# A decode attention block with a gated MLP: weight loads in fewer, longer pieces

## The chip, the cores and the metric

The kernel runs on one core of a Trainium2 chip. The core has five instruction queues: TensorE (PE, with its weight loads as PEld), VectorE (DVE), ScalarE (ACT), GpSimd (POOL) and SyncE (SP). Sixteen DMA engines move data between the chip's memory (HBM) and the on-chip memory (SBUF, 128 partitions). Transfers are put into DMA queues by SP, ACT and POOL. The metric is the device time of one launch in microseconds (us); smaller is better.

## The reference, cut to what matters

One token passes through two branches that a scalar gate mixes. Branch A is attention over a cache of 4096 keys and values for 32 heads of 128 numbers, with a projection before (wq) and after (wo). Branch B is an MLP with a squared ReLU. All inputs are bf16.

```python
g = sigmoid((x * gate_w).sum(-1))                     # x: 1 x 512
q = (x @ wq).reshape(32, 128)                         # wq: 512 x 4096
p = softmax(einsum("hd,hkd->hk", q, k_cache) * 128 ** -0.5)
o = einsum("hk,hkd->hd", p, v_cache)                  # caches: 32 x 4096 x 128
a = o.reshape(4096) @ wo                              # wo: 4096 x 512
h = relu(x @ w1 + b1) ** 2                            # w1: 512 x 1376
b = h @ w2 + b2                                       # w2: 1376 x 512
out = g * a + (1 - g) * b
```

The caches are 64 MB of the roughly 79 MB that must be read; wq and wo are 4 MB each, w1 and w2 1.4 MB each.

## The kernel before, in words

The kernel is written engine by engine with semaphores; no scheduler reorders it.

**The stream.** SP issues nearly all loads, in this order: wq in four transfers (L249, L257), keys of seven heads, and then in a loop over heads the values of head h and the keys of head h+7 (L268, L263). Each of those is 1 MB, 128 partitions of 8 KB. Eight buffers hold keys (Kt), eight hold values (Vt); from the ninth head on, SP waits until a buffer is free (L261, L262, L267) before it issues. After the values of head 8 it issues w1 in four transfers of 2752 bytes per partition (L286). Behind the last values come a part of wo (wob, wox) and w2 (w2a, w2b), L289 to L293.

**The work on a head.** DVE multiplies half of the keys with the query and sums (L631, sixteen instructions a head). PE transposes the other half (L428), ACT moves it out of PSUM (L362) and PE takes the scores (L439). A softmax over groups of four heads follows, and PE multiplies with the values (L464).

**The buffer W.** wq fills W, 128 partitions of 32 KB. Its product with x is made in eight steps spread over the first 22 heads (L406, semaphore s_qps). When the eighth is done, W is free, and 92 of its partitions are filled with 92 rows of wo of 32 KB each, enough for 23 heads. These loads are the strips. `place` turns a strip into a first partition, a step and a count of partitions.

- POOL issues the fourteen strips in `RUNS` (L319) after it has waited for s_qps: two of 24 rows, one of 3, one of 7 and ten of 2, 78 rows in all.
- SP issues the five strips in `FIRST` (L280) between the values of heads 20 to 24: four of 3 rows and one of 2, 14 rows.

The strips carry `max_dma_last_dim=8192`, which cuts a row of 32 KB into pieces of 8 KB. In the built program a strip of 24 rows then is a pattern of 24 x 4 x 4096 elements: two counting dimensions, rows and pieces, over a contiguous run.

**The turn.** The code keeps account of which DMA engine a strip's rows go to. `RUNS` names for each strip a first engine e and a number of engines k (4 and 12 for the 24-row strips, two rows each; 4 and 3; 7 and 2; 9 and 7, and so on). `turns` follows a cursor modulo 16: after a strip it stands at e + k. Where the next strip is to start elsewhere, a filler transfer of d tiny rows (L316, a pattern of d x 2 x 8 elements, 32 bytes a row) moves it on by d, or it is reset to zero (L313) and moved from there. `place` puts the rows of engine e into partitions 32+4e to 35+4e, or from 4e (engines 0 to 7) or 64+4e (engines 8 to 15), four each. So engine e always fills the same eight partitions.

**The end.** PE multiplies the strips with the attention result (L508), DVE takes nine of the 32 column blocks (L681), PE adds wob, wox, w2a and w2b to the sum `acc` (L526, L532, L547), and DVE, PE and SP finish and store the output.

## Time and profile before

| | before |
|---|---|
| time of three runs, us | 196.81, 196.83, 196.99 (median 196.83) |
| profiled execution, us | span 195.4; the page gives it no other time |
| DVE busy | 139.5 us, 71% |
| PE busy | 132.8 us, 68% |
| bytes read from HBM | 78.32 MB |
| mean rate of the DMA engines | 403 GB/s |
| last input lands (w2a) | 191.87 us after the span's start |

The span runs from the first to the last instruction; the median lies 1.4 us above it, which is what stands around the program on the chip. "Busy tenths" are the busy share in 40 equal slices of the span, 9 meaning 90% or more. A DMA line such as `x32, 1024.0 KB, 27.1` tells the number of transfers, the size of each, and the median us from issue to landing. The trace also holds a record of each packet on the DMA engines: queue, start, duration and size, but not which of the 16 engines it was.

### The profile page before, as it was taken

The numbers are of one execution on the slowest core, as the hardware profiler recorded it, in microseconds if no ns is written. First come the engines' busy times: TensorE is split into PE (matmuls) and PEld (weight loads), VectorE is DVE, ScalarE is ACT, GpSimd is POOL, SyncE is SP. The second block draws the span as 40 slices with busy tenths as digits, with TensorE's granted clock in tenths as the row PEclk, the third lists the DMA queues.
The fourth block names the chain that finished last, engine by engine and source line by source line (L and its number), as shares of the span: only waits on it lengthen the run. The fifth ranks groups of instructions, "written<-read, shape, count | busy, mean of one in ns | idle before, by whom it ended". The sixth has DMA issues, their size and how long they took to land.

```text
span 195.4 us, 6571 instructions
## 1 busy us (share of the span) xinstructions
PE 132.8 (68%) x2409; PEld 117.3 (60%) x2409; DVE 139.5 (71%) x1151; ACT 79.4 (41%) x148; POOL 29.9 (15%) x53
## 2 busy tenths in 40 slices
PE   0128657597986857906797771568998677787774
PEld 0106527476686647606667761568997667776664
DVE  0307999999998687707877773577769999958510
ACT  2105838456563536403347330633068333612000
POOL 2000000000000000000009950000089760000000
PEclk9999966667555665555555555555555555555555
DMA  6999999999999999999999999999999999999991
GB/s 227 420 426 424 424 418 424 411 421 426 416 411 423 418 421 407 420 421 421 418 421 419 411 416 416 406 409 413 408 419 421 426 409 421 419 423 414 416 382 57
DMA packets 12717, 78.76 MB, mean 403 GB/s; under 512 B 2489, under 2 KB 2715, under 8 KB 3356
## 3 DMA queue, kind: packets, MB, share of 16 engines
q1 hardware_dynamic: 11134, 75.77, 94.0%
q0 software_dynamic: 1536, 2.56, 3.5%
q8 instruction: 19, 0.31, 0.7%
q14 instruction: 14, 0.11, 0.2%
q10 hardware_dynamic: 14, 0.01, 0.0%
HBM read 78.32 MB, written 0.00 MB: 401 GB/s over the span
## 4 chain that ended last, share of the span: by engine, by line
DMA 59%; DVE 22%; PE 9%; SPq 6%; issue 3%; ACT 0%
DMA Kt<-in_A_k_cache_dram 42%; DVE Kt L631 19%; DMA w2a<-in_B_w_dram 12%; DMA W<-in_A_wq_dram 6%; SPq L268 4%; PE KP L428 3%; PE pX L482 2%; DVE S L631 1%; SPq L263 1%; PE pQ L406 1%; PE pX L478 1%; PE pX L547 1%; PE pS L439 1%; DVE dg L646 1%; DVE S L637 0%
## 5 line engine op out<-in xcount | busy, mean ns | idle before, releaser
L631 DVE CUSTOM_DVE_ANT_0 Kt<-Kt,qb 128x128 bf16<-128x128 bf16 x512 | 113.3, 290 | 23.4 <-DMA Kt<-in_A_k_cache_dram 23.4
L362 ACT ACTIVATE kT<-KP 128x1024 bf16<-128x1024 bf16 x64 | 61.8, 1021 | 68.4 <-PE KP L428 68.4
L428 PE MATMUL KP<-ident,Kt 128*128 128x128 bf16 x512 | 55.2, 294 | 32.0 <-DMA Kt<-in_A_k_cache_dram 32.0
L428 PEld LDWEIGHTS KP<-ident,Kt 128*128 128x128 bf16 x512 | 47.9, 137 | 34.4 <-DMA Kt<-in_A_k_cache_dram 33.6
L631 DVE DVE_READ_ACCUMULATOR2_ANT S<- 128x1 f32 x512 | 41.4, 81 | 0.0
L439 PE MATMUL pS<-qcol,kT 128*128 128x1 bf16 x512 | 19.0, 167 | 11.1 <-DVE S L637 11.1
L439 PEld LDWEIGHTS pS<-qcol,kT 128*128 128x128 bf16 x512 | 18.4, 106 | 13.2 <-DVE S L637 13.2
L316 POOL DMA_DIRECT2D xb<-in_B_w_dram x9 | 5.3, 592 | 100.3 <-PE pQ L406 100.3
L406 PE MATMUL pQ<-W,xb 128*128 128x512 bf16 x32 | 14.5, 609 | 6.4 <-DMA W<-in_A_wq_dram 6.4
L464 PEld LDWEIGHTS pO<-E,Vt 128*128 128x128 bf16 x512 | 15.4, 104 | 1.1 <-issue 0.8
L464 PE MATMUL pO<-E,Vt 128*128 128x1 bf16 x512 | 16.0, 165 | 0.0
L334 POOL TENSOR_SCALAR_AFFINE_SELECT w_sb<-w_sb 24x36 bf16<-24x36 bf16 (+5 forms) x19 | 11.0, 577 | 2.7
L354 ACT ACTIVATE qb<-pQ 128x512 bf16<-128x512 f32 x8 | 4.7, 591 | 14.8 <-PE pQ L406 14.8
L406 PEld LDWEIGHTS pQ<-W,xb 128*128 128x128 bf16 x32 | 3.6, 130 | 10.9 <-issue 10.9
L373 ACT ACTIVATE E<-S,nM 128x32 bf16<-128x32 f32 x32 | 9.9, 309 | 0.3
L464 PE MATMUL pQ<-E,Vt 128*128 128x1 bf16 x256 | 8.1, 165 | 2.3 <-DMA Vt<-in_A_v_cache_dram 2.0
L464 PEld LDWEIGHTS pQ<-E,Vt 128*128 128x128 bf16 x256 | 7.7, 104 | 2.6 <-issue 2.5
L464 PEld LDWEIGHTS pX<-E,Vt 128*128 128x128 bf16 x256 | 7.9, 105 | 0.7 <-issue 0.6
L464 PE MATMUL pX<-E,Vt 128*128 128x1 bf16 x256 | 8.1, 166 | 0.0
L319 POOL DMA_DIRECT2D W<-in_A_wo_dram x14 | 7.8, 563 | 0.0
L617 DVE CAST qcol<-pQ 128x4 bf16<-128x4 f32 x8 | 1.2, 152 | 8.5 <-PE pQ L414 8.5
L637 DVE COPY S<-pS 128x16 f32<-128x16 f32 x32 | 5.4, 169 | 2.2 <-PE pS L439 2.2
(85 smaller groups left out, 93.5 us busy)
## 6 DMA issues: line engine op xcount, KB each, us to landing
Kt<-in_A_k_cache_dram SPq DMA_DIRECT2D x32, 1024.0 KB, 27.1
Vt<-in_A_v_cache_dram SPq DMA_DIRECT2D x32, 1024.0 KB, 27.2
W<-in_A_wq_dram SPq DMA_DIRECT2D x4, 1024.0 KB, 7.8
W<-in_A_wo_dram POOLq DMA_DIRECT2D x2, 768.0 KB, 13.0
w_sb<-in_B_w_dram SPq DMA_DIRECT2D x4, 344.0 KB, 22.9
Kt<-in_A_wo_dram SPq DMA_DIRECT2D x1, 1024.0 KB, 21.5
w2a<-in_B_w_dram SPq DMA_DIRECT2D x1, 1024.0 KB, 23.4
W<-in_A_wo_dram POOLq DMA_DIRECT2D x10, 64.0 KB, 23.4
```

The costliest lines, as they stand in the source:

```text
L268: eng.dma_start(Vt[:, h % NV, :], v_h[h, :, :]).then_inc(s_v[h % NV], 16)
L316: eng.dma_start(dm[0:d, sent, :, 0:8], src[:, :, 0:8]).then_inc(s_dm[sent], 16)
L319: eng.dma_start(W[p:p + st * (k - 1) + 1:st, :], woa_v[q:q + k, :], max_dma_last_dim=8192).then_inc(s_wp[n], 16)
L334: eng.affine_select(out=part, in_=part, compare_op=ALU.not_equal, fill=1.0, base=-st * q, pattern=[[st, 4], [-1, st * (k - 1) + 1]], chann ...
L362: eng.activation(kT[:, h % 2, j * HB * 128:(j + 1) * HB * 128], KP[n % 3][:, :], ACT.Copy).then_inc(s_ev, 1)
L373: eng.activation(E[:, h % NE, :], S[:, h % NS, :], ACT.Exp, bias=nM[:, h:h + 1], scale=SCALE, accum_out=RS[:, h:h + 1]).then_inc(s_e, 1)
L406: mm = eng.matmul(pQ[:, :], xb[:, t, :], wq_sb[:, t, c * 512:(c + 1) * 512], start=(t == 0), stop=(t == 3))
L428: mm = eng.transpose(KP[n % 3][:, y * 128:(y + 1) * 128], Kt[:, h % NK, b * 128:(b + 1) * 128], ident[:, :])
L439: mm = eng.matmul(S2[:, y:y + 1], kT[:, h % 2, y * 128:(y + 1) * 128], qcol[:, h:h + 1], start=True, stop=True)
L464: mm = eng.matmul(O(h, h + 1), Vt[:, h % NV, b * 128:(b + 1) * 128], E[:, h % NE, b:b + 1], start=(b == 0), stop=(b == NB - 1))
L631: ins = eng.tensor_tensor_reduce(kb, kb, qb[:, h * 128:(h + 1) * 128], 1.0, 0.0, ALU.mult, ALU.add, S[:, h % NS, b:b + 1])
L637: eng.tensor_copy(S[:, h % NS, XB:NB], S2).then_inc(s_cp, 1)
```

## The change: what it does

Three groups of loads are issued with longer contiguous pieces. The bytes, their places in SBUF and the order of the transfers stay.

- wq: two transfers of 16 KB per partition in place of four of 8 KB; PE waits for two semaphores in place of four.
- w1: one transfer of 11,008 bytes per partition in place of four of 2752.
- the strips of wo, on POOL and on SP: no cap, so that each row is one piece of 32 KB. In the built program a strip of 24 rows is now 24 x 16384 elements: one counting dimension over a contiguous run. `RUNS`, `turns` and the fillers stay as they were.

```diff
-        nc.sync.dma_start(wq_sb[:, 0, :], wq_v[:, 0, :]).then_inc(s_wq[0], 16)
+        nc.sync.dma_start(wq_sb[:, 0:2, :], wq_v[:, 0:2, :]).then_inc(s_wq[0], 16)
...
-            for t in range(1, 4):
-                eng.dma_start(wq_sb[:, t, :], wq_v[:, t, :]).then_inc(s_wq[t], 16)
+            eng.dma_start(wq_sb[:, 2:4, :], wq_v[:, 2:4, :]).then_inc(s_wq[1], 16)
...
-                    eng.dma_start(W[p:p + st * (k - 1) + 1:st, :], woa_v[q:q + k, :],
-                                  max_dma_last_dim=8192).then_inc(s_wr, 16)
+                    eng.dma_start(W[p:p + st * (k - 1) + 1:st, :], woa_v[q:q + k, :]).then_inc(s_wr, 16)
...
-                    for t in range(4):
-                        eng.dma_start(w1_sb[:, t, :], w1_v[:, t, :]).then_inc(s_w1, 16)
+                    eng.dma_start(w1_sb[:, :, :], w1_v[:, :, :]).then_inc(s_w1, 16)
...
-                eng.dma_start(W[p:p + st * (k - 1) + 1:st, :], woa_v[q:q + k, :],
-                              max_dma_last_dim=8192).then_inc(s_wp[n], 16)
+                eng.dma_start(W[p:p + st * (k - 1) + 1:st, :], woa_v[q:q + k, :]).then_inc(s_wp[n], 16)
...
-                eng.wait_ge(s_w1, 64)
+                eng.wait_ge(s_w1, 16)
```

More of the change, by code (lines that the diff above doesn't have):

```diff
@@ L195, in bass_gated_mix__gqa_block_cached__dense_activation_squared_relu__decode_kernel @@
         s_b = sem("s_b")
-        s_wq = [sem(f"s_wq{t}") for t in range(4)]
+        s_wq = [sem(f"s_wq{t}") for t in range(2)]
         s_w1 = sem("s_w1")
@@ L396, in _ @@
             eng.matmul(Z, onesf[0:1, :], zp[:, :], start=True, stop=True).then_inc(s_z, 1)
-            for t in range(4):
+            for t in range(2):
                 eng.wait_ge(s_wq[t], 16)
```

## The prediction

> **What bounds the kernel now.** I read the page's rows for DMA by slices and queues first, then a table of five stretches, then the end of the chain, then DMA issues and the waits.

> ```profile
> span 195.4 us, 6571 instructions
> ...
> DMA  6999999999999999999999999999999999999991
> ...
> DMA packets 12717, 78.76 MB, mean 403 GB/s; under 512 B 2489, under 2 KB 2715, under 8 KB 3356
> ...
> q1 hardware_dynamic: 11134, 75.77, 94.0%
> q0 software_dynamic: 1536, 2.56, 3.5%
> q8 instruction: 19, 0.31, 0.7%
> q14 instruction: 14, 0.11, 0.2%
> ```

> All sixteen DMA engines work through 38 of 40 slices. Queue 1 is what SP issues, queue 0 what POOL issues (2.56 MB: its 78 rows of wo). Queues 8 and 14 fetch instructions: 19 packets of 16 KB and, mostly, packets of 8 KB.

> ```profile
> core 0: us, PE busy (x) PEld busy (x) DVE busy (x) ACT busy (x) POOL busy (x), PEclk, DMA share, GB/s
> 0.00:13.00 13.00, 0.84 (x6) 0.70 (x6) 1.93 (x10) 1.83 (x4) 1.25 (x9) 1.00 0.87 350
> 13.00:102.00 89.00, 64.06 (x1018) 52.41 (x1019) 72.98 (x662) 44.73 (x72) 0.00 (x0) 0.63 1.01 419
> 102.00:146.00 44.00, 31.70 (x565) 30.72 (x566) 29.28 (x248) 17.59 (x34) 16.60 (x25) 0.50 1.02 413
> 146.00:189.50 43.50, 33.30 (x744) 31.06 (x741) 34.74 (x229) 15.27 (x39) 12.09 (x20) 0.50 1.01 417
> 189.50:195.40 5.90, 2.86 (x82) 2.46 (x81) 0.54 (x3) 0.00 (x0) 0.00 (x0) 0.50 0.31 100
> ```

> DMA share is 1.01 or 1.02 in each stretch from 13 to 189.5 us, at 413 to 419 GB/s, while DVE and PE leave a fifth to a third free. The limit is the service time of the DMA engines.

> ```profile
> 168.51 23.36 DMA w2a<-in_B_w_dram
> 191.87 0.14 issue
> 192.01 0.99 PE pX L547 x32
> ```

> The chain ends with an input that was issued 23.4 us before it landed, so it stood in a queue; 3.5 us of work follow. The packet records show how the engines finish: about 16 packets are in flight until 189.7 us, about 9 at 191.0, four at 192.0, and the last data packet ends at 192.56. Some four engines set the end, 2.8 us behind the first to finish. So the question is what the change does to the busiest engine.

> ```profile
> Kt<-in_A_k_cache_dram SPq DMA_DIRECT2D x32, 1024.0 KB, 27.1
> Vt<-in_A_v_cache_dram SPq DMA_DIRECT2D x32, 1024.0 KB, 27.2
> W<-in_A_wq_dram SPq DMA_DIRECT2D x4, 1024.0 KB, 7.8
> ```

> Keys and values wait in the queue for most of 27 us: no issue instruction is on the path.

> **Part 1, wq and w1.** The packet records give the price of a piece: median 46 ns for 1 KB, 109 for 2752 bytes, 312 for 8 KB. That is a line of 37 ns per KB and about 7 ns per piece. Each engine serves 8 of the 128 partitions, so wq falls from 32 pieces to 16 on an engine and w1 from 32 to 8: 40 pieces x 7 ns = 0.28 us less. Five transfers fewer, each with a closing record of 9 ns on every engine, give 0.05. SP issues two wq transfers fewer, some 0.4 us each in its timeline, and three w1 transfers fewer of 0.4 to 2.1 us; that is worth nothing, since the keys behind wq queue up anyway (SP's first value transfer already takes 2.07 us to issue) and 23 to 27 us of backlog cover w1. If the cover were gone it would be a gain of under 1 us at the start. PE needed all four parts of wq before its first product, so two semaphores cost nothing; the same holds for w1.

> Pieces of data over 8 KB are not in the trace. The nearest rows are the instruction queues: 0.7% x 16 x 195.4 us / 19 = 1.15 us per packet of 16 KB, 0.2% x 16 x 195.4 / 14 = 0.45 us per packet of 8 KB. So the two ends are 0.62 us for 16 KB (the line) and about 1.1 us (that row). By the second, wq costs 16 x (1.09 - 0.62) = +7.4 us on each engine. I take the line: three sizes of data lie on it, and instruction packets come singly and go to another place.

> **Part 2, the strips: the price of a piece.** A row now is one piece, not four: 3 x 7 ns less per row. POOL's 312 packets of 8 KB took 97.9 us together, 0.314 each, so a row is 1.256 us of one engine's time.

> **Part 3, the strips: which engine.** This decides. By the kernel's own account (first engine e, number of engines, two rows each in the 24-row strips) engine 0 now carries 3 POOL rows and 5 SP rows, engine 1 two and five, engines 7, 8 and 15 eight rows each and the others one to six. Eight rows, 10.0 us, is the most, on four engines, and four engines end last. The trace agrees with the account where it can: in the first 0.35 us of strip data twelve 8 KB packets of queue 0 start, the 12 engines of the first strip.

> That account was kept for strips with two counting dimensions, rows and pieces. The fillers have two as well, 2 x 8 out of rows of 16, which cannot fold into one although 32 bytes would need no second. After the change the strips have one. No POOL transfer with one is in this trace, so I bound it. At one end it is dealt as before: with eight rows on the busiest engine the whole change is -(40 + 24) x 7 ns - 0.05 = -0.5 us. At the other end the cursor plays no part and every POOL strip starts at engine 0. Engines 0 and 1 then get 2 + 2 rows of the 24-row strips, 1 of the 3-row, 1 of the 7-row and 10 of the 2-row strips: 16, plus their 5 from SP: 21. The excess over eight is 13 x 1.256 = 16.3 us, less (40 + 63) x 7 ns and 0.05 for the shorter lists, 0.8: +15.5 us. I take the second end: the fillers' odd shape makes sense only if the dealing depends on the second dimension.

> [...]

> **Part 4, the strips: whose partitions.** Engine 1's sixteen POOL rows then all go to partitions that the code gives to other engines (4 to those of engine 5, and so on), and those engines write keys and values there at the same time. The trace has one load that does not keep to the map: w2b, 96 partitions, six to an engine in order. While it lands, at 190.0 to 190.3 us, packets of 1 KB take up to 91 ns, not 46 (1.98 times), and packets of 2 KB 129 on average, not 84 (1.53 times). So a row out of place costs between nothing more and 0.98 x 1.256 us more. Engine 1 had seven rows, so its 14 more give the same 16.3 over the old end. Sixteen rows at 1.53: + 16 x 0.53 x 1.256 = 10.6 us; at 1.98: +19.7. I take 1.53, a mean over that stretch.

> Sum: 16.3 + 10.6 - 0.8 = +26.1 us. The tail of 3.5 us and the 1.4 us between span and median stay. On the profiled 195.4 that is 221.5; on the median of 196.83 it is 222.9, say 223. Can it hide? Other engines would wait, not help: a key transfer counts as landed when its last engine is done. DVE and PE stall there and, with 20 to 35% free, keep up again afterwards; engine 1 always has the backlog. The strips are first read at 175.6 us, long after they land.

> **Rivals.** (a) The dealing stays, and only piece prices change: 196.83 - 0.5 = 196.3, faster. For it: same bytes, same order, the whole 0.5 us on the busiest engine. Against: the shape of the fillers. It decides if the engine with most rows keeps eight. Its gain is near what measurement tells, 0.2% or 0.4 us, so a third of this case falls within that. [...]

> (b) The strips pile up, but rows out of place cost nothing extra: 196.83 + 15.5 = 212.3. For it: the slow packets at 190 us could be due to the mix of small packets. It is the low part of my case.

> (c) The dealing stays, but long pieces run like the 16 KB instruction packets, 0.068 us per KB: wq +7.4, eight rows 8 x (2.17 - 1.25) = +7.4, w1 8 x (0.73 - 0.44) = +2.3; together 214. Against: the line through three sizes.

> **How the numbers follow.** Piled up, with any price for rows out of place: 0.84, from 212 to 232 by part 4, with a us or three beyond each end for the count of rows that the busiest engine had before; that is its own range, 209 to 236. Rival (b) is 0.2 of that. Rival (c): 0.03. Rival (a): 0.13, of which 0.09 is faster by over 0.2% and 0.04 within 0.2%. Slower: 0.84 + 0.03 = 0.87. The range 209 to 236 leaves out (a) and some 0.07 for long pieces on top of the pile or a higher price.

> **What would show it.** DMA packets fall by some 1000 (256 of wq, 384 of w1, 276 of strips and closing records). The DMA share falls clearly below 1 in the part after 107 us, because fourteen engines wait for two; the mean rate falls from 403 to about 350 GB/s. The waits of DVE L631 and PE L428 for keys (23.4 and 32.0 us) each grow by about the whole loss, behind 107 us and not before. Queue 0 shows packets far above 1.25 us per 32 KB if rows out of place cost. The first product starts at 13.2 us as before; if it starts near 20, long pieces are slow in themselves. Wrong would be: a DMA share that stays at 1 to the end with a time near 196.

## The result and the profile after

The changed kernel takes 230.43 us (median of four runs, 230.35 to 230.88), the kernel before 196.91 us beside it. The ratio is 1.1705, with a 95% interval of 1.1688 to 1.1721: 33.5 us slower. The forecast was 223 us, from 209 to 236.

The page of the changed kernel, its rows for DMA:

```profile
span 228.9 us, 6565 instructions
...
DMA  6999999999999999999999999989999999696100
GB/s 238 447 408 422 421 420 420 420 418 422 412 420 421 421 415 424 420 420 368 274 259 222 256 372 322 372 302 367 358 384 378 361 399 358 256 412 244 56 40 16
DMA packets 11187, 78.76 MB, mean 344 GB/s; under 512 B 1875, under 2 KB 2101, under 8 KB 2230
...
q1 hardware_dynamic: 10372, 75.77, 85.6%
q0 software_dynamic: 768, 2.56, 4.6%
```

The bytes are the same. The rate is that of before, around 420 GB/s, for 18 slices, and then falls, to 222 GB/s in slice 22. The engines nevertheless look busy there: until slice 35 most digits are 9. Queue 0, POOL's, moves the same 2.56 MB, but its packets occupy 4.6% of 16 x 228.9 us, 168 us, where before 3.5% of 16 x 195.4 us made 109 us. So between 105 and 155 us the engines are busy at work that got slower, and at the end most of them have nothing to do. A table by stretches shows the two:

```profile
core 0: us, PE busy (x) PEld busy (x) DVE busy (x) ACT busy (x) POOL busy (x), PEclk, DMA share, GB/s
107.00:157.00 50.00, 13.93 (x265) 13.50 (x265) 16.54 (x149) 9.15 (x17) 8.18 (x15) 0.50 0.98 293
157.00:207.00 50.00, 34.20 (x625) 32.59 (x625) 36.22 (x287) 18.29 (x34) 15.65 (x21) 0.50 0.95 368
207.00:226.20 19.20, 14.03 (x381) 13.32 (x382) 7.76 (x16) 1.50 (x9) 0.00 (x0) 0.50 0.22 82
```

The first stretch is POOL's strips: a DMA share of 0.98, but 293 GB/s. In the last 19 us the share is 0.22. The packet records have two to three packets in flight on average from 210 to 219 us and about one at 222; the last data packet ends at 226.0 us. From 221 us on it is one engine: followed back packet by packet, it works without a gap to 226.0 us, mostly at 309 ns a piece of 8 KB.

SP's own strips tell which engines are late. By the code's account their 14 rows go to engines 0 and 1 (five each) and 2 (four). The 14 packets of 32 KB form three series: one of four that starts at 158.5 us, and two of five that start at 171.0 and 175.7. In the kernel with a cap of 16 KB on POOL's strips (below) the three series start within 1.6 us, at 140.0 to 141.5. So engines 0 and 1 stand 12.5 and 17 us behind engine 2, in one order or the other.

The chain ends as before, with w2a:

```profile
199.51 25.71 DMA w2a<-in_B_w_dram
225.22 0.14 issue
225.35 0.99 PE pX L543 x32
```

The waits for keys take up the whole loss; DVE waits 32.6 us more than before and PE 35.5. Two lines of the kernel before, then two of the changed one:

```profile
PE KP L428 <- DMA Kt<-in_A_k_cache_dram: 32.0, 19, 4.5
DVE Kt L631 <- DMA Kt<-in_A_k_cache_dram: 23.4, 14, 5.4
...
PE KP L424 <- DMA Kt<-in_A_k_cache_dram: 67.5, 18, 13.8
DVE Kt L627 <- DMA Kt<-in_A_k_cache_dram: 56.0, 16, 13.8
```

The first product with wq starts at 13.23 us, before at 13.20.

The packet records price the new pieces. From SP, a piece of 16 KB of wq takes 611 ns (median), one of w1 (11,008 bytes) 416 and a whole row of 32 KB 1213, all close to the line of the prediction. From POOL, the same 32 KB take 2032 ns on average and 2118 in the median, up to 2312. Yet four of POOL's 78 take only 1218 to 1312; of three strips (partitions 1, 2 and 3) the first row lies, by the code's account, with engine 0 itself. The fourth is the last row of all, and why it is fast was not looked for. Twelve of POOL's rows start together at 106.7 to 107.1 us, twelve more at 109.1 to 109.8: a strip of 24 rows is on twelve engines. From 129 to 157 us there are at most two POOL packets in flight, 18 in all: the last nine strips of two rows.

### The profile page after: what moved, and what is told of

Same layout as the page of the kernel before. It is cut to its first block, busy times and chain, and to the rows that moved or that the text cites. A ratio compares the mean times of both kernels' runs of the same rounds, so it can differ in the third digit from the quotient of the medians.

```text
span 228.9 us, 6565 instructions
## 1 busy us (share of the span) xinstructions
PE 132.5 (58%) x2409; PEld 117.4 (51%) x2409; DVE 138.8 (61%) x1151; ACT 79.5 (35%) x148; POOL 29.9 (13%) x53
## 2 busy tenths in 40 slices
DMA packets 11187, 78.76 MB, mean 344 GB/s; under 512 B 1875, under 2 KB 2101, under 8 KB 2230
## 3 DMA queue, kind: packets, MB, share of 16 engines
q1 hardware_dynamic: 10372, 75.77, 85.6%
q0 software_dynamic: 768, 2.56, 4.6%
## 4 chain that ended last, share of the span: by engine, by line
DMA 63%; DVE 16%; SPq 13%; PE 6%; issue 2%; ACT 0%
DMA Kt<-in_A_k_cache_dram 46%; DVE Kt L627 14%; DMA w2a<-in_B_w_dram 11%; DMA W<-in_A_wq_dram 5%; SPq L279 5%; SPq L267 4%; SPq L262 4%; PE KP L424 2%; PE pQ L402 2%; PE pO L460 1%; DVE S L627 1%; PE pX L543 1%; PE pS L435 1%; PE pM L449 0%; DVE S L633 0%
## 5 line engine op out<-in xcount | busy, mean ns | idle before, releaser
L313 POOL DMA_DIRECT2D xb<-in_B_w_dram x9 | 5.9, 653 | 100.3 <-PE pQ L402 100.3
L460 PEld LDWEIGHTS pO<-E,Vt 128*128 128x128 bf16 x512 | 15.5, 104 | 1.1 <-issue 0.8
L322 POOL MEMSET w_sb<- 24x3072 bf16 x1 | 2.6, 2648 | 54.8 <-PE pX L478 54.8
L316 POOL DMA_DIRECT2D W<-in_A_wo_dram x14 | 7.2, 516 | 0.0
## 6 DMA issues: line engine op xcount, KB each, us to landing
Kt<-in_A_k_cache_dram SPq DMA_DIRECT2D x32, 1024.0 KB, 28.2
Vt<-in_A_v_cache_dram SPq DMA_DIRECT2D x32, 1024.0 KB, 29.2
Kt<-in_A_wo_dram SPq DMA_DIRECT2D x1, 1024.0 KB, 23.7
w2a<-in_B_w_dram SPq DMA_DIRECT2D x1, 1024.0 KB, 25.7
```

The lines of the kernel that those rows point to most:

```text
L316: eng.dma_start(W[p:p + st * (k - 1) + 1:st, :], woa_v[q:q + k, :]).then_inc(s_wp[n], 16)
L460: mm = eng.matmul(O(h, h + 1), Vt[:, h % NV, b * 128:(b + 1) * 128], E[:, h % NE, b:b + 1], start=(b == 0), stop=(b == NB - 1))
```

## The experiments

The dealing theory: POOL's strips with one counting dimension are dealt from engine 0 on, regardless of the cursor; engines 0 and 1 carry 21 rows each and write most of them into partitions that other engines are filling. The rivals: long pieces are slow in themselves; the parts add up; place does not matter. The kernel before was timed beside each run, at 196.9 to 197.0 us.

**wq and w1 alone.** The edits to L249 to L257 and L286 of the change, and nothing else.

> Only wq (two transfers) and w1 (one transfer) are changed; all strips keep the cap of 8 KB. Dealing theory (the loss comes from POOL's strips being dealt from engine 0 on): 40 pieces fewer on each engine at 7 ns and five closing records at 9 ns, -0.33 us, so 196.6 beside 196.9. Rival (long pieces are slow in themselves or upset the stream): wq and w1 are long here too, so 198 or more, the first product after 14 us.

Measured: 196.96 us, ratio 0.9999 (0.9990 to 1.0008). Long pieces do no harm, and the first product starts on time, but the gain of 0.33 us is not there. In the packet records w1 takes 0.18 us less per engine. For wq nothing is gained: its last piece ends at 12.59 us, before at 12.52; the first pieces take 0.7 to 1.4 us each in place of 0.3 to 1.0.

**POOL's strips at 16 KB.** The change, with

```diff
-                eng.dma_start(W[p:p + st * (k - 1) + 1:st, :], woa_v[q:q + k, :]).then_inc(s_wp[n], 16)
+                eng.dma_start(W[p:p + st * (k - 1) + 1:st, :], woa_v[q:q + k, :],
+                              max_dma_last_dim=16384).then_inc(s_wp[n], 16)
```

> The change, but POOL's strips with a cap of 16 KB in place of none, so that they keep two counting dimensions (rows x 2 pieces of 16 KB). SP's strips are uncapped. Dealing theory: the account of engines holds again, POOL packets of 16 KB take about 0.62 us, the busiest engines save 40 + 16 to 24 pieces: -0.5 us, 196.4, DMA share 1 to 189 us. Rival (length of POOL's pieces): half the length, about half the loss, 210 to 215.

Measured: 196.73 us, ratio 0.9989 (0.9980 to 0.9997). All of the 33.5 us is gone while POOL's pieces are twice as long as before. They take 0.622 us, no more than two of 8 KB. Its page has the DMA row of the kernel before, and POOL's queue takes nearly the share that it took there (3.5%):

```profile
DMA  6999999999999999999999999999999999999991
...
q0 software_dynamic: 1024, 2.56, 3.4%
```

This kernel differs from the change in the length of POOL's pieces and in the second counting dimension; the columns kernel below tells the two apart. It is also the only kernel here whose interval lies below 1, by 0.2 us, less than half of what was expected.

**POOL's strips alone.** Only L319 loses its cap.

> Only POOL's strips lose their cap; wq, w1 and SP's strips are as before. Dealing theory: all of the loss and the small savings of the other parts absent: 230.4 + 0.3 for wq and w1 + 0.1 for SP's strips = 230.8. Rival (the parts add up, each with a share of the loss): clearly under 229.

Measured: 230.47 us, ratio 1.1704 (1.1683 to 1.1726). This one edit is the whole loss; that wq, w1 and SP's strips save anything beside it cannot be seen.

**Columns: one counting dimension with short pieces.**

```diff
-                eng.dma_start(W[p:p + st * (k - 1) + 1:st, :], woa_v[q:q + k, :],
-                              max_dma_last_dim=8192).then_inc(s_wp[n], 16)
+                for c in range(4):
+                    eng.dma_start(W[p:p + st * (k - 1) + 1:st, 4096 * c:4096 * c + 4096],
+                                  woa_v[q:q + k, 4096 * c:4096 * c + 4096]).then_inc(s_wp[n], 16)
```

The two waits for `s_wp` go from 16 to 64.

> POOL's strips issued as four transfers each, one for each 8 KB column of the rows: pieces stay at 8 KB, but each transfer has one counting dimension. All else as before. Dealing theory: the rows land on the same engines as with the change, POOL packets of 8 KB take about 0.5 us (2.03 / 4), and the time is that of pool_only plus 21 x 3 x 7 ns = 0.4 and up to 1 us for 42 more closing records: 230.5 to 232. Rival (length of POOL's pieces): the pieces are as before, so 197 to 199.

Measured: 227.69 us, ratio 1.1563 (1.1542 to 1.1584). The loss is there with pieces of 8 KB, so length is not its cause. The page's row for POOL's queue (packets, MB, share of 16 engines):

```profile
q0 software_dynamic: 2208, 2.57, 4.1%
```

And stretches of the same kernel, with the columns as above:

```profile
107.00:157.00 50.00, 25.35 (x446) 24.55 (x447) 24.29 (x218) 13.02 (x21) 28.59 (x56) 0.50 1.02 323
157.00:207.00 50.00, 25.46 (x520) 24.26 (x517) 28.70 (x221) 15.27 (x36) 12.50 (x21) 0.50 0.92 356
207.00:224.00 17.00, 12.10 (x328) 11.40 (x327) 7.14 (x13) 0.65 (x5) 0.00 (x0) 0.50 0.14 54
```

It is the picture of the change: a full DMA share at a low rate, then a tail at 0.14. The time is 2.8 us below the strips of 32 KB and outside the expected range. POOL's packets take 0.407 us, less than a quarter of 2.03: short pieces in the wrong place cost their writer less.

**No fillers.** The changed kernel, with `turns` returning no filler.

```diff
-            out.append((False, d) if d != 1 else (True, e))
+            out.append((False, 0))
```

> The changed kernel without its nine filler transfers, so that whatever cursor there is stands elsewhere at each strip. Dealing theory (a strip with one counting dimension starts at engine 0 whatever the cursor says): 230.4, at most 0.3 less for nine transfers fewer. Rival (the strips still follow the cursor and only the number of engines differs): the rows lie on other engines, and the time moves by several us either way.

Measured: 230.75 us, ratio 1.1718 (1.1692 to 1.1745), the same as the change. Without fillers a cursor would stand at 0, 12, 8 and 11 for the first four strips, not at 4, 4, 4 and 7. The time does not move with it, and the three series of SP's long rows start within 0.5 us of where they do in the change: these strips with one counting dimension do not use it.

**One engine earlier.** The kernel before, with its account off by one, so that the first filler has three rows.

```diff
-        at, out = 0, []
+        at, out = 1, []
```

> The kernel before, with the first filler of three rows in place of four: every strip of POOL starts one engine earlier, so that nearly all of POOL's rows go to partitions of the next engine, while the most rows on an engine stay eight (three engines) and pieces stay at 8 KB. It prices a row out of place alone. By the rows of the changed kernel (32 KB in 2.03 us, not 1.256): eight rows cost 8 x 0.78 = 6.2 us on engines 6 and 7, and engine 7 is disturbed as long again by engine 6's eight rows in its partitions: 203 to 209, POOL packets at about 0.5 us. Rival (place does not matter, the 32 KB packets were slow for their length): 196.9, POOL packets at 0.314.

Measured: 211.99 us, ratio 1.0780 (1.0754 to 1.0805): 15.1 us slower, beyond the expected 6 to 12. A table of stretches, with the same columns; the first line is the kernel before, the others this one:

```profile
107.00:157.00 50.00, 35.74 (x644) 34.22 (x644) 36.98 (x296) 20.23 (x36) 21.10 (x30) 0.50 1.02 415
...
107.00:157.00 50.00, 25.37 (x446) 24.57 (x447) 24.27 (x218) 13.02 (x21) 10.50 (x17) 0.50 1.02 341
157.00:196.00 39.00, 28.04 (x616) 26.94 (x613) 33.87 (x228) 15.92 (x39) 12.97 (x20) 0.50 1.01 417
196.00:207.00 11.00, 8.52 (x212) 8.01 (x213) 1.98 (x6) 0.00 (x0) 0.00 (x0) 0.50 0.38 144
```

The engines are fully busy (1.02) at 341 GB/s while the strips load, and at 417 GB/s afterwards. Nothing but the place of the rows (and which engines carry the odd row) differs from before. The packet records say what got slower. POOL's 312 packets took 130.2 us in place of 97.9, which is 0.41 us more per row of 32 KB. SP's packets of 8 KB, nine in ten of them keys and values, took 2959.5 us in place of 2848.2, which is 1.43 us per row. Engine 7 writes eight rows out of place and receives engine 6's eight. If the engine that writes pays the first and the owner of the partitions the second, engine 7 loses 8 x (0.41 + 1.43) = 14.7 us, near the 15.1 measured.

A record does not name its engine, so this division is argued, not shown, and the records of the changed kernel speak against so clean a one. There a row out of place ends at 154.2 us, and the SP packet that starts at that moment, most likely the same engine's next, takes 641 ns, while of the 52 that start from 152.7 to 154.2 us 49 take at most 330: so the writer pays in its next packet too. And while the two rows of another strip are in flight together, from 129.4 to 131.3 us, 54 SP packets of 8 KB start, and 40 of them take over 450 ns. Two writers and two owners can start at most five such packets each in that time, 20 in all, so other engines are slowed as well. What is shown is that place alone costs; how the cost is divided stays open. The expectation put 6.2 us on each of the two sides; the loss is larger than both together.

**More rows in place.** The kernel before loads the four strips of engines 7 and 8 once more; four fillers bring the cursor there, and the later waits count both loads.

```diff
+            ran = sent
+            for n, d in zip((3, 5, 9, 12), (6, 14, 14, 14)):
+                eng.wait_ge(s_wp[n], 16)
+                src = B_w1[0:d, 0:32].rearrange("p (a c) -> p a c", a=2)
+                eng.dma_start(dm[0:d, sent, :, 0:8], src[:, :, 0:8]).then_inc(s_dm[sent], 16)
+                sent += 1
+                p, st, k, q = STRIPS[n]
+                eng.dma_start(W[p:p + st * (k - 1) + 1:st, :], woa_v[q:q + k, :],
+                              max_dma_last_dim=8192).then_inc(s_wp[n], 16)
```

> The kernel before, with the four strips of POOL that go to engines 7 and 8 loaded a second time, to the same partitions: four rows more on two of the busiest engines, in place, with the cursor moved there by four more fillers. It prices the pile alone. Dealing theory: 4 x 1.256 = +5.0 us, 201.9, if engines 7 and 8 are among the last, up to 1 less if they are not quite. Rival (an engine's surplus is taken up by slack elsewhere): under 198.

Measured: 200.89 us, ratio 1.0203 (1.0187 to 1.0218), 4.0 us more for 5.0 us of rows. Stretches of this kernel, with the same columns:

```profile
107.00:157.00 50.00, 32.41 (x583) 31.33 (x580) 36.66 (x290) 18.32 (x35) 25.26 (x37) 0.50 1.02 412
157.00:189.50 32.50, 23.17 (x507) 22.23 (x508) 23.98 (x157) 10.65 (x26) 3.26 (x9) 0.50 1.01 417
189.50:197.00 7.50, 6.11 (x181) 5.70 (x179) 0.80 (x4) 0.00 (x0) 0.00 (x0) 0.50 0.36 127
```

Nothing got slower: 412 GB/s while the strips load, and POOL's packets at 0.315 us. But a surplus on two of sixteen engines comes through to the end nearly in full, as a tail at a share of 0.36. Engines 7 and 8 seem to have been about 1 us from being last.

**The long strips in place.** The changed kernel with another set of strips: four of 16 rows, uncapped, whose row j lies in a partition of engine j, and smaller ones with the 16 KB cap for the rest.

```diff
+    RUNS = [(INNER, 0, 16, 0, 1), (INNER, 0, 16, 1, 1), (INNER, 0, 16, 2, 1), (INNER, 0, 16, 3, 1),
+            (OUTER, 4, 3, 0, 1), (SEAM, 7, 2, 0, 1), (OUTER, 9, 6, 0, 1), (WRAP, 15, 2, 1, 1),
+            (OUTER, 1, 2, 1, 1), (SEAM, 7, 2, 1, 1), (WRAP, 15, 2, 2, 1), (OUTER, 1, 2, 2, 1),
+            (SEAM, 7, 2, 2, 1), (WRAP, 15, 2, 3, 1)]
+    FIRST = [(OUTER, 0, 3, 0, 1)]
...
+                              **({} if k == 16 else {"max_dma_last_dim": 16384})).then_inc(s_wp[n], 16)
```

> All long pieces of the change are kept for wq, w1, SP's one strip and for 64 of POOL's rows: four uncapped strips of 16 rows, whose row number j lies in partitions of engine j (partitions 32 to 95 in steps of 4). The other 25 rows of POOL keep two counting dimensions (cap of 16 KB) and the cursor. Dealing theory: a strip with one counting dimension is dealt one row to an engine from engine 0 on, so every row is in place, POOL packets of 32 KB take 1.22 us and not 2.03, and no engine has more than eight rows; engine 3 has four in place of one. So the loss is gone: 196.6 to 198.5. Rival (32 KB pieces from POOL's queue are slow or misplaced whatever the partitions): 64 of 78 such rows remain, 210 or more.

Measured: 200.07 us, ratio 1.0152 (1.0139 to 1.0165). Stretches of this kernel, with the same columns:

```profile
107.00:157.00 50.00, 33.54 (x591) 32.55 (x592) 34.99 (x288) 18.40 (x35) 17.54 (x22) 0.50 1.01 417
157.00:189.50 32.50, 24.06 (x558) 23.13 (x556) 24.90 (x159) 10.54 (x26) 2.92 (x6) 0.50 1.01 414
189.50:196.00 6.50, 4.19 (x121) 3.73 (x122) 0.60 (x3) 0.00 (x0) 0.00 (x0) 0.50 0.21 70
```

Thirty of the 33.5 us are gone with 64 rows still uncapped. Sixteen of POOL's packets of 32 KB start together at 105.8 to 106.2 us, and all 64 take 1.213 to 1.227 us. The rate stays at 417 GB/s. So these strips with one counting dimension are dealt to the engines from 0 on, and a row that lies where the code's account has its engine costs the plain price (SP's rows of 32 KB take 1.213 us in the change). The other 3.1 us are more than expected. They are a tail at a DMA share of 0.21, with about one packet in flight from 192 us on. Engine 3, which has four rows here and had one before, would be 3 x 1.22 = 3.7 us later; what else keeps it as busy as the others in the kernel before was not looked for.

**Balance.** The kernel with the 16 KB cap, with one strip moved from engines 15 and 0 to 9 and 10.

```diff
-            (SEAM, 7, 2, 3, 1), (WRAP, 15, 2, 3, 1)]
+            (SEAM, 7, 2, 3, 1), (OUTER, 9, 2, 1, 1)]
```

> The kernel with the 16 KB cap for POOL, in which the last strip, one row each on engines 15 and 0 (eight rows each), is replaced by one with a row each on engines 9 and 10 (five rows each). If engines 15 and 0 are the last to finish, the end comes earlier by what they lead engines 7 and 8, which the extra rows put at some 1.0 us (4 x 1.256 cost 4.0): 195.7 to 196.0. If other engines end last: 196.7 as before that edit. If engines 9 and 10 are nearly full for another reason: up to 197.5.

Measured: 197.10 us, ratio 0.9999 (0.9988 to 1.0010). No gain, so the first case falls: engines 15 and 0 are not alone in ending last. The other two cases are not told apart.

## Why the prediction was right, point by point

**The bound.** Right. The path ends in w2a's landing with the same tail, and the engines of the chip that compute wait for keys. Most rows of the page that were named moved as named: the rate fell to 344 GB/s (about 350 was said), the waits for keys grew by about the loss. The DMA share did not: it was to fall clearly below 1 behind 107 us, but was 0.98 to 157 us and 0.95 to 207, and fell to 0.22 only then. Fourteen engines did not so much wait for two as work more slowly, since a slow packet counts as busy (a share of 0.98 at 293 GB/s from 107 to 157 us, where the kernel before has 1.02 at 415); the term for it is in part 4. The count of packets fell by 1530, not by some 1000: POOL's closing records fell too, which was not counted.

**Part 1, wq and w1: -0.3 us.** The line for longer pieces is right (611 ns for 16 KB against 0.62 us). The instruction packets were no measure: 19 of them came one at a time, at 1086 ns on average, and where they go no run shows. The saving did not reach the time. Alone it measures 0.0 us, with an interval of about 0.2 either way. For wq the reason shows in the packets: at the start of the stream a longer first piece takes longer (0.7 to 1.4 us in place of 0.3 to 1.0), and the last ends no earlier (at 12.59 us, before at 12.52).

**Part 3, which engine: +15.5 us.** Right, and shown by four kernels, and by SP's late rows on engines 0 and 1: POOL's strips alone are the loss (230.47 us); a second counting dimension at 16 KB removes it (196.73); one counting dimension at 8 KB brings it back (227.69); the cursor does not matter (230.75 without fillers). The choice of this end was an inference from the fillers' shape. The packets show how many engines a strip takes: 24 rows start on twelve engines (106.7 to 107.1 us in the change), 16 rows on sixteen (105.8 to 106.2 us with the long strips in place). The 15.5 us itself is a count of rows times their price. Only a smaller pile was measured alone: four rows more in place cost 4.0 us for 5.0 us of rows.

**Part 4, whose partitions: +10.6 us.** That rows out of place cost time was right (15.1 us with the rows one engine earlier), this term too small; that is why 26.1 us were forecast and 33.5 came. It had two faults. A row of 32 KB out of place took 2.065 us (158.5 us of POOL packets, less three in place, over 75 rows), not 1.53 x 1.256 = 1.92; one in place took 1.216. So sixteen rows on engine 1 make 16 x (2.065 - 1.216) = 13.6 us. And the term put at nothing what the rows do to other packets. From 105 to 155 us SP's 8 KB packets took 153 us more than 312 ns each, before 9 us; over 75 rows that is 1.9 us per row, more than the row itself lost.

How much of this falls on engine 1 is open. If the owner of the partitions alone pays, engine 1, which owns those of two rows that engine 0 writes, loses 3.8 us. With 21 x 1.216 - 8 x 1.256 = 15.5 us for the pile the sum is 15.5 + 13.6 + 3.8 = 32.9 us, beside 33.5 measured. If all sixteen engines share it alike, it is 144 / 16 = 9.0 us, and the sum is 38.1. The records speak against the first, as told above, and in the kernel that deals one engine earlier the second would make 8 x 0.41 + 111 / 16 = 10.3 us, not 15.1. So the nearness of the first sum is no proof.

There is luck in the 1.53, which came from packets of 2 KB beside w2b. Of w2b the trace shows six packets between two closing records (188.67 to 188.92 and 188.81 to 189.06 us, on the two engines that come to it first), where the code's account would give an engine eight or four; which partitions they fill it does not show. The factor measured here is 2.065 / 1.216 = 1.70 in one piece, but 1.30 for pieces of 8 KB in the columns kernel (0.407 us over 0.314) and 1.33 one engine earlier.

Which partitions belong to which engine is the code's account, and no record shows it partition by partition. The runs agree with it as far as this: moving nearly all of POOL's rows one group away costs 15.1 us, and 64 rows of 32 KB placed by it take 1.213 to 1.227 us each, where the change has 2.032 on average.

**The rivals.** (a), the dealing stays, fell: it is what the 16 KB cap does, at 196.73 us, and the change takes 230.43. (b), rows out of place cost nothing, fell with the kernel that deals one engine earlier, at 211.99 us. (c), long pieces run like instruction packets, fell with the first kernel, at 196.96 us.

**What stays open.** The columns kernel loses 30.8 us. Its pile of 16.3 us, 16 x 0.39 for the writer (POOL's packets 126.9 us in place of 97.9, over 75 rows) and 2 x 2.5, if the owner alone pays what SP's 8 KB packets lose (187 us), make 27.5. Where the other 3.3 us lie was not found, nor why the long strips in place still cost 3.1 us, nor which engine is last in the kernel before.

## What to carry to other kernels

Here all DMA engines were full (a share of 1.01 or 1.02 from 13 to 189.5 us in the kernel before), and work added to two of them came through to the end nearly in full: 4.0 us for 5.0 us of rows. The edit left bytes and order alone and still moved rows between engines: for POOL's transfers here the shape of the pattern in the built program decided that, 196.73 us with two counting dimensions, 227.69 to 230.75 with one on the same strips. So look at the counting dimensions of a POOL transfer before and after an edit, and at GB/s beside the DMA share: here a share of 1.02 at a rate that fell from 415 to 341 GB/s meant packets that got slower, and a share that fell to 0.36 in a tail (the kernel with four rows more) meant a pile. Longer pieces than 8 KB were worth at most 0.2 us of 197 here.
